# The V loads of an attention and two-MLP kernel, issued by GpSimd's queue instead of SyncE's

## The chip, the cores and the metric

The kernel runs on one core of one Trainium2 chip. The metric is the device time of one execution in microseconds (us), and shorter is better. Engines are named TensorE (PE), VectorE (DVE), ScalarE (ACT), GpSimd (POOL) and SyncE (SP). SyncE does no arithmetic here: it issues DMAs.

## The reference, cut to what matters

Chunked attention over 4 batch rows, 8 heads, 768 tokens and 64 dimensions, then two MLPs on the 3072 x 512 result, all in fp32:

```python
# per chunk c of 32 queries: 16 keys to the left, 8 to the right, 8 memory tokens in front
k_full = concat([mem_k, k[:, :, l_start:r_end]]); v_full = concat([mem_v, v[:, :, l_start:r_end]])
scores = q_c @ k_full.T / sqrt(D)
a = exp(scores - max(scores)); a = a / (sum(a) + 1e-9)
out[:, :, c] = a @ v_full
...
x = out.transpose(0, 2, 1, 3).reshape(3072, 512)
r = maximum(x @ w_in, 0)                                   # 512 -> 2048
x = (s * r * r + b) @ w_out                                # 2048 -> 512
g = x @ w_gate                                             # 512 -> 1536
y = (g * sigmoid(g) * (x @ w_val)) @ w_out2                # 1536 -> 512
```

## The kernel before

**Tiling.** The attention runs in 24 groups g of 128 queries (4 chunks, all 8 heads), six groups (GB) to a batch row. Three groups make one token tile of 384, which goes through the first MLP in slices W0 to W15 of 128 hidden units: `hp` is the slice's first product, `r` its ReLU, `ghi` and `glo` the two parts of s*r*r + b, `acc` the second product. fp32 accuracy comes from splitting each operand into a hi and a lo part and taking three matmuls for one (`product`, L559 to L562): hi weights times hi data, hi weights times lo data, lo weights times hi data, in this order. The third one needs the lo part of the weights.

**A slice of weights.** W15, for example, is 1 MB in two DMAs (L240 and L245, into a tile raw_first15 of the pool of "w" slots), then a split: a magnitude (L840 on ScalarE), two short VectorE steps (L846, L850), two long ones (L855, L862), the hi copy (L231) and lo (L904). The first 150 us hold the splits of all sixteen slices, beside the attention of the first groups.

**q and k.** The first six groups load whole token rows (`load_tokens`, L285) and transpose on TensorE (psQ, psK). Later ones load 36 to 44 small DMAs of 32 rows (`load_quadrant`, L327 to L350): K8 is the loads of group 8, into the tiles `kin` (one buffer for all groups) and `qin`. VectorE transposes them in blocks of 32 x 32: `qt` (L356) for queries, `kT` (L362) for keys. The next group's loads into kin wait for kT.

**V.** `load_values` (L378 to L405) writes a group's windows of V into one of two buffers, v0 or v1 by the group's parity: eight DMAs of 56 KB, ten or twelve at a batch row's ends. For the first two groups of a batch row it also loads the 8 rows of mem_v and copies them over the chunks with six GpSimd copies (L392). psV, or psB in later groups, is the matmul of the probabilities with V.

**What sets the order.** A planner (`Plan`, L63 to L143) simulates tasks with a cost each and starts, on every engine, the ready task with the longest way behind it; the instructions are then written in that order. A transfer is a task of SyncE (0.45 us for each DMA) followed by a task for the movement (`transfer`, L826). `LOADS` fixes the order of the first loads on SyncE: "W0 K0 W1 V0 K1 K2 W2 V1 W4 V2 ...". `plan_queries` (L929 to L956) places a group's loads. TensorE's order is written by hand (`START`, `VISITS`). Every engine runs its instructions strictly in order, and a DMA on SyncE waits for the one eight places ahead of it.

Of the kernel before, what the change touches and what calls it, by code (L numbers as in the profile page):

```python
# [41 lines left out]
}  # L42

LOADS = (
    "W0 K0 W1 V0 K1 K2 W2 V1 W4 V2 K3 W3 V3 K4 W6 K5 W5 V4 W8 V5 W7 W10 W9 "
)

MOVED = (
# [98 lines left out]
def attention_and_two_mlps(  # L147
# [21 lines left out]
    nc = tc.nc  # L169
    B, H, S, D = q.shape  # L170
    NT, DM = out.shape
    NMEM = mem_k.shape[2]
# [7 lines left out]
    GB = S // GQ  # L180
    T = 3 * GQ
    NC = GQ // CHUNK
    WIN = LEFT + CHUNK + RIGHT
    KC = NMEM + WIN
# [169 lines left out]
    def turn_queries(g):  # L354
        staged[g] = {"qt": ap_.tile([P, NP, GQ], F32, tag="qt", name=f"qt{g}")}
        nc.vector.transpose(  # L356
            out=staged[g]["qt"].rearrange("p j s -> p (j s)"), in_=loaded[g]["q"].rearrange("p j n i -> p (j n i)")
        )
# [19 lines left out]
    def load_values(g):  # L378

        b, gi = divmod(g, GB)  # L380
        s0 = gi * GQ
        n = g % 2
        if n not in v_bufs:
            v_bufs[n] = ld.tile([P, NC, NP, D], F32, tag=f"v{n}", name=f"v{n}")
        tv = v_bufs[n]
        for e in range(2):
            p0 = e * KC
            if gi < 2:
                mem = tv[p0:p0 + NMEM]
                nc.sync.dma_start(out=mem[:, 0], in_=mem_v[b, e:H:2].rearrange("h s d -> s h d"))  # L390
                for c in range(1, NC):
                    nc.gpsimd.tensor_copy(mem[:, c], mem[:, 0])  # L392
            for c in range(NC):
                a = s0 + c * CHUNK - LEFT
                left, over = max(0, -a), max(0, a + WIN - S)
                for row, first, n in (
                    (0, 0, left), (left, a + left, WIN - left - over), (WIN - over, S - over, over)
                ):
                    if n:
                        r0 = p0 + NMEM + row  # L400
                        nc.sync.dma_start(
                            out=tv[r0:r0 + n, c],
                            in_=v[b, e:H:2, first:first + n, :].rearrange("h s d -> s h d"),
                        )
        loaded.setdefault(g, {})["v"] = tv  # L405

    def bank(pool, tag, name):
# [393 lines left out]
    def second_store(h, s, i):  # L801
# [7 lines left out]
    plan = Plan(  # L809
        dict(w=SLOTS - LENT, wt=SLOTS - 2, fly=2),  # L810
        dict(
            sc=LENT, f=2, own=1, qk=1, v=2, kT=1, kt=1, qt=1, at=1, on=1, x=2, r=4, ghi=2, glo=2, acc01=1,
            acc2=1, acc3=1, a=2, h=2, yq=1, so=1, z=5, a1=1, a2=1, a3=1, v1=2, v2=1,
        ),
    )
# [10 lines left out]
    def transfer(deps, emit, n, kilobytes, get=(), take=(), give=(), rate=380.0, name=None):  # L826

        issue = issues[name] = plan.add(SP, 0.45 * n, emit, deps, [*get, "fly"], take=take)
        return plan.add(MOVE, kilobytes / rate, None, [issue], put=["fly"], lag=1.8, give=give)

    def split(landed, raw, key, pool, name, done, put=("w",), sums=False):

        held = {}
# [95 lines left out]
    def plan_queries(g, early):  # L929
        vv = None  # L930
        if g >= EARLY:
            qk = None
            for a in range(12):
                qk = transfer(
                    [issues[f"K{g}_{a - 1}"]] if a else [], lambda a=a: load_quadrant(g, *divmod(a, 3)), 4 if a % 3 else 1,
                    64 if a % 3 else 14, take=["qk"] if a == 0 else (), rate=100.0, name=f"K{g}_{a}",
                )
                if a == 5:
                    vv = transfer([], lambda: load_values(g), 8, 460, take=["v"], rate=180.0, name=f"V{g}")
            t = plan.add(DVE, 0.60, lambda: turn_queries(g), [qk], take=["qt"])  # L940
            at_[g] = {"v": vv, "qt": t}
            t = plan.add(DVE, 0.72, lambda: turn_keys(g), [t], take=["kT"], give=["qk"])
            t = plan.add(ACT, 0.82, lambda: spread_keys(ACT, g, False), [t], take=["kt"])
            t = either(f"m{g}", {ACT: 0.26, DVE: 0.20}, lambda e: spread_keys(e, g, True), [t], give=["kT"])
            at_[g]["t"] = at_[g]["qt"], t
            return
        qk = transfer(
            [], lambda: load_tokens(g), 4, 590, take=["sc"], rate=180.0, name=f"K{g}"
        )
        vv = transfer([], lambda: load_values(g), 8, 460, take=["v"], rate=180.0, name=f"V{g}")  # L950
        at_[g] = {"v": vv, "qk": qk}
        t = plan.add(PE, 0.44, lambda: stage_queries(g, early), [qk], take=["acc2"] if early else ["a"])
        at_[g]["qt"] = either(
            f"q{g}", {ACT: 0.50, DVE: 0.60}, lambda e: stage_queries_copy(e, g), [t], take=["qt"],
            give=["acc2"] if early else ["a"],
        )  # L956
# [277 lines left out]
    for item in START.split():  # L1234
        what, g = item[0], int(item[1:] or 0)
# [100 lines left out]
```

## Time and profile before

| | |
|---|---|
| device time, median of 3 runs | 1234.26 us (1233.92 to 1235.15) |
| profiled execution | 1235.41 us, of which the span is 1233.6 us |
| mean granted TensorE clock | 0.989 |
| TensorE busy (PE) | 1189.7 us, 96% of the span |
| VectorE busy | 773.4 us, 63% |
| ScalarE busy | 506.3 us, 41% |
| GpSimd busy | 22.8 us, 2% |
| V loads | 208 DMAs: 176 of 56 KB and, at a batch row's ends, 8 each of 48, 40, 16 and 8 KB; 16 more of mem_v, 8 KB each |

TensorE is the busiest engine, so what counts is where it waits: nearly all of it lies in the first 106 us, in which the weights are split and the first groups' attention runs. The loads of V end before 570 us. A row of the timeline reads: start, length, engine, line, operation, output <- input, count, and in brackets the idle time of the engine ahead of it with what ended it.

### The profile page before, as it was taken

To read this page: it belongs to the slowest core of one execution; us is meant where nothing else is said; L and a number is where in the kernel's file an instruction comes from. 1 tells how busy PE (TensorE), PEld (TensorE's weight loads), DVE (VectorE), ACT (ScalarE), POOL (GpSimd) and SP (SyncE) were. 2 spreads that over 40 slices of the span, in tenths; PEclk is the share of its full clock that TensorE was granted. 3 is DMA by queue.
4 is the path that set the end of the run, shared out by engine and by line. 5 is a ranking of instruction groups with operands and counts; after the bars stand their busy time and mean duration, and the time that the engine had idled before them with its cause. 6 is when DMAs were issued, how large, how long until landed. Compare 5 with 4: busy or idle time off the path is not lost.

```text
span 1233.6 us, 25831 instructions
## 1 busy us (share of the span) xinstructions
PE 1189.7 (96%) x10296; PEld 1129.8 (92%) x10296; DVE 773.4 (63%) x1496; ACT 506.3 (41%) x1018; POOL 22.8 (2%) x54
## 2 busy tenths in 40 slices
PE   3788999999999999999999999999999999999998
PEld 3677999999999999999999999999999999999997
DVE  5899975556445444543679886658864448744444
ACT  2455433331334333333367555445543335433332
POOL 1001100000000000000000000000000000000000
PEclk9799999999999999999999999999999999999999
DMA  8956442223222232230462555567755458554532
GB/s 191 219 120 190 104 123 43 62 52 67 44 51 63 42 67 45 51 91 1 156 219 96 187 198 188 188 227 282 263 187 187 183 182 299 207 186 188 188 114 93
DMA packets 217128, 174.11 MB, mean 141 GB/s; under 512 B 157487, under 2 KB 188719, under 8 KB 215471
## 3 DMA queue, kind: packets, MB, share of 16 engines
q1 hardware_dynamic: 217006, 172.45, 45.1%
q8 instruction: 81, 1.33, 0.4%
q14 instruction: 41, 0.33, 0.1%
HBM read 124.40 MB, written 47.97 MB: 140 GB/s over the span
## 4 chain that ended last, share of the span: by engine, by line
PE 79%; SPq 9%; DMA 6%; DVE 3%; issue 2%; ACT 1%; DVEq 0%; ACTq 0%
PE chain_a L560 6%; PE chain_a L561 6%; PE chain_a L562 6%; PE oacc L561 5%; PE oacc L560 5%; PE oacc L562 5%; PE acc L560 5%; PE acc L561 5%; PE acc L562 5%; PE hp L560 5%; PE hp L562 5%; PE hp L561 5%; PE chain_b L561 4%; PE chain_b L562 4%; PE chain_b L560 4%; SPq L350 3%
## 5 line engine op out<-in xcount | busy, mean ns | idle before, releaser
L560 PE MATMUL acc<-ghi,w_first 128*128 128x384 f32 x512 | 176.0, 344 | 3.0 <-DVE ghi L231 1.8
L560 PE MATMUL hp<-xhi,w_first 128*128 128x384 f32 x512 | 175.7, 343 | 0.7 <-ACT xhi L229 0.7
L561 PE MATMUL acc<-glo,w_first 128*128 128x384 f32 x512 | 173.2, 338 | 2.5 <-DVE glo L622 1.1
L561 PE MATMUL hp<-xlo,w_first 128*128 128x384 f32 x512 | 172.6, 337 | 1.1 <-DVE xlo L553 1.1
L562 PE MATMUL hp<-xhi,w_first 128*128 128x384 f32 x512 | 172.5, 337 | 0.0
L562 PE MATMUL acc<-ghi,w_first 128*128 128x384 f32 x512 | 172.3, 337 | 0.0
L748 ACT ACTIVATE kept<-chain_a 128x256 f32<-128x256 f32 x216 | 83.0, 385 | 163.4 <-PE chain_a L562 134.4
L600 DVE SCALAR_TENSOR_TENSOR r<-r,s_sb 128x384 f32<-128x384 f32 x92 | 57.0, 620 | 107.8 <-ACT r L589 105.1
L589 ACT ACTIVATE r<-hp 128x384 f32<-128x384 f32 x96 | 47.1, 491 | 186.1 <-PE hp L562 179.1
L560 PE MATMUL oacc<-w_down,ghi 128*128 128x512 f32 x288 | 114.1, 396 | 0.1
L561 PE MATMUL oacc<-w_down,ghi 128*128 128x512 f32 x288 | 114.1, 396 | 0.0
L562 PE MATMUL oacc<-w_down,glo 128*128 128x512 f32 x288 | 112.0, 389 | 0.0
L560 PEld LDWEIGHTS acc<-ghi,w_first 128*128 128x128 f32 x512 | 96.8, 189 | 5.9 <-DVE ghi L231 2.8
L561 PEld LDWEIGHTS acc<-glo,w_first 128*128 128x128 f32 x512 | 97.0, 189 | 5.4 <-DVE glo L620 3.1
L560 PEld LDWEIGHTS hp<-xhi,w_first 128*128 128x128 f32 x512 | 97.3, 190 | 2.2 <-ACT xhi L229 0.9
L561 PEld LDWEIGHTS hp<-xlo,w_first 128*128 128x128 f32 x512 | 97.4, 190 | 1.3 <-DVE xlo L553 1.3
L562 PEld LDWEIGHTS hp<-xhi,w_first 128*128 128x128 f32 x512 | 97.1, 190 | 0.0
L562 PEld LDWEIGHTS acc<-ghi,w_first 128*128 128x128 f32 x512 | 96.8, 189 | 0.0
L765 DVE TENSOR_TENSOR v<-v,g 128x256 f32<-128x256 f32 x144 | 61.0, 424 | 52.3 <-ACT g L761 50.4
L753 DVE TENSOR_TENSOR v<-chain_b,kept 128x256 f32<-128x256 f32 x144 | 61.0, 423 | 41.5 <-PE chain_b L562 26.8
L773 DVE TENSOR_TENSOR glo<-v,ghi 128x256 fp32r<-128x256 f32 x144 | 60.6, 421 | 36.6 <-ACT ghi L229 36.6
L560 PE MATMUL chain_a<-y,hi_up 128*128 128x256 f32 x288 | 81.3, 282 | 0.6 <-ACT kept L748 0.5
(137 smaller groups left out, 2689.4 us busy)
## 6 DMA issues: line engine op xcount, KB each, us to landing
y<-ops_dram SPq DMA_DIRECT2D x48, 512.0 KB
ops_dram<-y SPq DMA_DIRECT2D x24, 512.0 KB
sum_dram<-o SPq DMA_DIRECT2D x48, 256.0 KB
o<-sum_dram SPq DMA_DIRECT2D x12, 1024.0 KB
v<-in_v_dram SPq DMA_DIRECT2D x176, 56.0 KB
yhi<-ops_dram_hi SPq DMA_DIRECT2D x12, 768.0 KB
ylo<-ops_dram_lo SPq DMA_DIRECT2D x12, 768.0 KB
raw_first<-in_moe_w_in_dram SPq DMA_DIRECT2D x16, 512.0 KB
```

Source lines behind the costliest of these rows:

```text
L350: nc.sync.dma_start(out=qin[:, j], in_=q[b, h, s0:s0 + GQ, ds].rearrange("(n t) i -> t n i", t=QUAD))
L560: nc.tensor.matmul(o, whi, xhi, start=first, stop=False, skip_group_check=onto)
L561: nc.tensor.matmul(o, whi, xlo, start=False, stop=False, skip_group_check=onto)
L562: nc.tensor.matmul(o, wlo, xhi, start=False, stop=last, skip_group_check=onto)
L589: nc.scalar.activation(out=r, in_=hp, func=AF.Relu)
L600: nc.vector.scalar_tensor_tensor(out=r, in0=r, scalar=s_sb[:, 0:1], in1=r, op0=ALU.mult, op1=ALU.mult)
L748: nc.scalar.activation(out=t, in_=st2[n]["A"], func=AF.Copy)
L753: nc.vector.tensor_tensor(out=t, in0=st2[n]["B"], in1=st2[n].pop(f"a{i}"), op=ALU.add)
L765: nc.vector.tensor_tensor(out=v, in0=v, in1=g, op=ALU.mult)
L773: nc.vector.tensor_tensor(out=lo, in0=st2[n].pop(f"v{half + 1}"), in1=st2[n][f"hi{half}"].bitcast(F32), op=ALU.subtract)
```

## The change

All DMAs of `load_values` are issued by `nc.gpsimd`. GpSimd's copies of mem_v move behind the DMAs of their group. The planner no longer counts V as a transfer of SyncE: a new function `load_v` makes it a task of POOL with 1.0 us for each DMA, and a movement of its own; the V names leave `LOADS`.

```diff
--- before.py
+++ after.py
@@ -42,7 +42,7 @@
 }
 
 LOADS = (
-    "W0 K0 W1 V0 K1 K2 W2 V1 W4 V2 K3 W3 V3 K4 W6 K5 W5 V4 W8 V5 W7 W10 W9 "
+    "W0 K0 W1 K1 K2 W2 W4 K3 W3 K4 W6 K5 W5 W8 W7 W10 W9 "
 )
 
 MOVED = (
@@ -387,9 +387,7 @@
             p0 = e * KC
             if gi < 2:
                 mem = tv[p0:p0 + NMEM]
-                nc.sync.dma_start(out=mem[:, 0], in_=mem_v[b, e:H:2].rearrange("h s d -> s h d"))
-                for c in range(1, NC):
-                    nc.gpsimd.tensor_copy(mem[:, c], mem[:, 0])
+                nc.gpsimd.dma_start(out=mem[:, 0], in_=mem_v[b, e:H:2].rearrange("h s d -> s h d"))
             for c in range(NC):
                 a = s0 + c * CHUNK - LEFT
                 left, over = max(0, -a), max(0, a + WIN - S)
@@ -398,10 +396,14 @@
                 ):
                     if n:
                         r0 = p0 + NMEM + row
-                        nc.sync.dma_start(
+                        nc.gpsimd.dma_start(
                             out=tv[r0:r0 + n, c],
                             in_=v[b, e:H:2, first:first + n, :].rearrange("h s d -> s h d"),
                         )
+        for e in range(2 if gi < 2 else 0):
+            mem = tv[e * KC:e * KC + NMEM]
+            for c in range(1, NC):
+                nc.gpsimd.tensor_copy(mem[:, c], mem[:, 0])
         loaded.setdefault(g, {})["v"] = tv
 
     def bank(pool, tag, name):
@@ -827,6 +829,11 @@
 
         issue = issues[name] = plan.add(SP, 0.45 * n, emit, deps, [*get, "fly"], take=take)
         return plan.add(MOVE, kilobytes / rate, None, [issue], put=["fly"], lag=1.8, give=give)
+
+    def load_v(g):
+        edge = 4 * (g % GB == 0) + 2 * (g % GB in (1, GB - 1))
+        issue = plan.add("POOL", 1.0 * (8 + edge), lambda: load_values(g), take=["v"])
+        return plan.add("MOVE_V", 0.1, None, [issue], lag=2.0)
 
     def split(landed, raw, key, pool, name, done, put=("w",), sums=False):
 
@@ -936,7 +943,7 @@
                     64 if a % 3 else 14, take=["qk"] if a == 0 else (), rate=100.0, name=f"K{g}_{a}",
                 )
                 if a == 5:
-                    vv = transfer([], lambda: load_values(g), 8, 460, take=["v"], rate=180.0, name=f"V{g}")
+                    vv = load_v(g)
             t = plan.add(DVE, 0.60, lambda: turn_queries(g), [qk], take=["qt"])
             at_[g] = {"v": vv, "qt": t}
             t = plan.add(DVE, 0.72, lambda: turn_keys(g), [t], take=["kT"], give=["qk"])
@@ -947,7 +954,7 @@
         qk = transfer(
             [], lambda: load_tokens(g), 4, 590, take=["sc"], rate=180.0, name=f"K{g}"
         )
-        vv = transfer([], lambda: load_values(g), 8, 460, take=["v"], rate=180.0, name=f"V{g}")
+        vv = load_v(g)
         at_[g] = {"v": vv, "qk": qk}
         t = plan.add(PE, 0.44, lambda: stage_queries(g, early), [qk], take=["acc2"] if early else ["a"])
         at_[g]["qt"] = either(
```

The planner places other work in answer. On SyncE at the start, the first rows behind W0 and K0 (numbers at a name's end tell buffers apart; v0 is group 0's V, qk1 the rows of group 1). Before:

```order
L240 DMA raw_first1_162<-in_moe_w_in_dram 128x4x256
L245 DMA raw_first1_162<-in_moe_w_out_dram 128x1024
L390 DMA v0_167<-in_mem_v_dram 8x4x64
L401 DMA v0_167<-in_v_dram 16x4x64
L401 DMA v0_167<-in_v_dram 40x4x64
L401 DMA v0_167<-in_v_dram 56x4x64 x3
```

And after:

```order
L240 DMA raw_first1_181<-in_moe_w_in_dram 128x4x256
L245 DMA raw_first1_181<-in_moe_w_out_dram 128x1024
L285 DMA qk1_186<-in_mem_k_dram 8x8x64
L285 DMA qk1_186<-in_k_dram 72x8x64
L285 DMA qk1_186<-in_q_dram 128x8x64
L285 DMA qk1_186<-in_k_dram 80x8x64
```

V0 is gone from between W1 and K1, the rows of group 1.

The V loads stand on GpSimd instead, from the program's start; these are its first rows after the change:

```order
masks.py:197 MEMSET ident_81 128x128
L390 DMA v0_156<-in_mem_v_dram 8x4x64
masks.py:199 ISA
masks.py:199 AFFINE_SELECT ident_81<-ident_81 128x128
L399 DMA v0_156<-in_v_dram 16x4x64
L399 DMA v0_156<-in_v_dram 40x4x64
L399 DMA v0_156<-in_v_dram 56x4x64 x3
```

Before, GpSimd held nothing there but the identity's making and the copies of mem_v.

On SyncE in the middle of the loads of group 8 (kin and qin8), where W15 (raw_first15) is issued. Before, where 14 of the group's 36 loads stand ahead of W15:

```order
L346 DMA kin_872<-in_k_dram 32x4x32
L350 DMA qin8_1855<-in_q_dram 32x4x32
L240 DMA raw_first15_1936<-in_moe_w_in_dram 128x4x256
L245 DMA raw_first15_1936<-in_moe_w_out_dram 128x1024
L346 DMA kin_872<-in_k_dram 32x4x32
```

And after, where 27 of the 36 stand ahead:

```order
L346 DMA kin_503<-in_k_dram 32x4x32
L350 DMA qin8_1866<-in_q_dram 32x4x32
L240 DMA raw_first15_2009<-in_moe_w_in_dram 128x4x256
L245 DMA raw_first15_2009<-in_moe_w_out_dram 128x1024
L327 DMA kin_503<-in_k_dram 24x4x32
```

W15 has moved back by 13 loads of group 8.

On VectorE at the end of the weights' splits: w_first15 is W15's hi (CAST) and lo (TENSOR_TENSOR), on6 the attention's output of group 6, psS7 and sc7 the scores of group 7, qt8 and kT8 the transposes of group 8. Before:

```order
L531 TENSOR_TENSOR on6_2085<-psV6_1_2023,rc6_1932 128x4x64
L622 SCALAR_TENSOR_TENSOR glo_2088<-r_2012,b_sb_87,ghi_2081 128x384
L231 CAST w_first15_2132<-raw_first15_1936 128x1024
L600 SCALAR_TENSOR_TENSOR r_2083<-r_2083,s_sb_86 128x384
L904 TENSOR_TENSOR w_first15_2132<-raw_first15_1936,w_first15_2132 128x1024
L622 SCALAR_TENSOR_TENSOR glo_2150<-r_2083,b_sb_87,ghi_2142 128x384
L468 TENSOR_REDUCE mx7_2165<-psS7_0_2098 128x4
L468 TENSOR_REDUCE mx7_2165<-psS7_1_2099 128x4
L481 TENSOR_TENSOR sc7_2170<-psS7_0_2098,mx7_2165 128x4x64
L481 TENSOR_TENSOR sc7_2170<-psS7_1_2099,mx7_2165 128x4x64
L356 STREAM_TRANSPOSE qt8_2173<-qin8_1855 128x512
L362 STREAM_TRANSPOSE kT8_2176<-kin_872 128x640
```

And after (L853, L857, L862 and L869 are the old L846, L850, L855 and L862):

```order
L483 TENSOR_TENSOR sc7_2141<-psS7_0_2082,mx7_2129 128x4x64
L483 TENSOR_TENSOR sc7_2141<-psS7_1_2083,mx7_2129 128x4x64
L624 SCALAR_TENSOR_TENSOR glo_2149<-r_2116,b_sb_87,ghi_2131 128x384
L853 TENSOR_SCALAR t_first15_2143<-t_first15_2143 128x1024
L857 TENSOR_SCALAR t_first15_2143<-t_first15_2143 128x1024
L862 SCALAR_TENSOR_TENSOR raw_first15_2009<-raw_first15_2009,t_first15_2143 128x1024
L869 SCALAR_TENSOR_TENSOR raw_first15_2009<-raw_first15_2009 128x1024
L356 STREAM_TRANSPOSE qt8_2156<-qin8_1866 128x512
L231 CAST w_first15_2158<-raw_first15_2009 128x1024
L362 STREAM_TRANSPOSE kT8_2160<-kin_503 128x640
L911 TENSOR_TENSOR w_first15_2158<-raw_first15_2009,w_first15_2158 128x1024
```

W15's split, done before sc7 in the old order, begins behind sc7 in the new one and ends behind kT8. TensorE's rows stand in the same order in both kernels.

## Rows read from the trace of the kernel before

**Rows 1.** Stretches: busy us of PE, PEld, DVE, ACT, POOL; PEclk; DMA share; GB/s.
```profile
0.00:60.00 60.00, 33.12 (x560) 28.30 (x561) 43.12 (x78) 19.87 (x31) 5.00 (x18) 0.86 0.87 201
60.00:150.00 90.00, 81.60 (x803) 75.57 (x802) 86.07 (x136) 46.07 (x70) 8.46 (x12) 0.96 0.54 147
150.00:270.00 120.00, 119.83 (x1290) 116.57 (x1289) 74.27 (x152) 38.93 (x67) 0.00 (x0) 1.00 0.31 68
276.00:280.00 4.00, 4.00 (x17) 4.00 (x16) 0.56 (x1) 1.35 (x3) 0.55 (x2) 0.61 0.30 55
```

**Rows 2.** Timeline near 274 us, TensorE and VectorE: start, length, operation, [idle before <-releaser].
```profile
274.56 0.44 PE L560 MATMUL acc<-ghi,w_first 128*128 128x384 f32 x1 [1.63 <-DVE ghi L231]
...
272.23 0.71 DVE L356 STREAM_TRANSPOSE qt<-qin 128x512 f32<-128x512 f32 x1 [3.33 <-DMA v<-in_mem_v_dram]
```

**Rows 3.** SyncE's queue ahead of that wait.
```profile
245.71 4.21 SPq L401 DMA_DIRECT2D v<-in_v_dram  x10
...
270.20 0.43 SPq L350 DMA_DIRECT2D qin<-in_q_dram  x1
```

**Rows 4.** TensorE in the first 50 us.
```profile
18.50 1.09 PE L415 MATMUL psQ<-ident,qk 128*128 128x128 f32 x4 [5.59 <-DMA qk<-in_q_dram]
19.38 1.06 PE L495 MATMUL psA<-ident,qk 128*128 128x128 f32 x4
42.53 1.26 PE L511 MATMUL psV<-v,at 64*32 64x64 f32 x64 [0.78 <-DVE at L231]
```

**Rows 5.** SyncE's queue in the first 40 us.
```profile
14.80 0.46 SPq L285 DMA_DIRECT2D qk<-in_q_dram  x1
29.81 7.36 SPq L401 DMA_DIRECT2D v<-in_v_dram  x8
```

**Rows 6.** ScalarE, group 0's exponential.
```profile
14.87 0.63 ACT L488 ACTIVATE qk<-qk 128x512 f32<-128x512 f32 x1 [1.28 <-DVE qk L481]
```

**Rows 7.** VectorE from 141 to 197 us, the steps around W15, kT and qt.
```profile
141.02 0.75 DVE L481 TENSOR_TENSOR sc<-psS,mx 128x256 f32<-128x256 f32 x2
145.37 0.83 DVE L362 STREAM_TRANSPOSE kT<-kin 128x640 f32<-128x640 f32 x1
159.95 0.69 DVE L846 TENSOR_SCALAR t_first<-t_first 128x1024 f32<-128x1024 f32 x1 [2.24 <-ACT t_first L840]
165.41 0.69 DVE L231 CAST w_first<-raw_first 128x1024 fp32r<-128x1024 f32 x1
166.54 1.22 DVE L904 TENSOR_TENSOR w_first<-raw_first,w_first 128x1024 fp32r<-128x1024 f32 x1
169.53 0.71 DVE L356 STREAM_TRANSPOSE qt<-qin 128x512 f32<-128x512 f32 x1
170.15 0.81 DVE L362 STREAM_TRANSPOSE kT<-kin 128x640 f32<-128x640 f32 x1
...
190.13 0.20 DVE L526 RECIPROCAL rc<-rc 128x8 f32<-128x8 f32 x1
196.39 0.70 DVE L356 STREAM_TRANSPOSE qt<-qin 128x512 f32<-128x512 f32 x1
```

**Rows 8.** SyncE's queue: K8's first load, W15's second, K8's last.
```profile
146.23 0.30 SPq L327 DMA_DIRECT2D kin<-in_k_dram  x1
153.86 0.50 SPq L245 DMA_DIRECT2D raw_first<-in_moe_w_out_dram  x1
166.06 0.43 SPq L350 DMA_DIRECT2D qin<-in_q_dram  x1
```

**Rows 9.** ScalarE, W15's magnitude.
```profile
158.80 1.12 ACT L840 ACTIVATE t_first<-raw_first 128x1024 f32<-128x1024 f32 x1 [1.74 <-DMA raw_first<-in_moe_w_out_dram]
```

**Rows 10.** TensorE, the first product with W15's lo.
```profile
168.35 0.33 PE L562 MATMUL hp<-xhi,w_first 128*128 128x384 f32 x1
```

**Rows 11.** GpSimd's copies over the span (ns: min/median/max); VectorE beside one.
```profile
L392 POOL COPY v<-v x48: 386/393/1408, 12.4 to 447.5; 8x256 f32<-8x256 f32 x48
...
114.44 1.41 DVE L862 SCALAR_TENSOR_TENSOR raw_first<-raw_first 128x1024 uint32<-128x1024 uint32 x1
```

## The prediction

> **What bounds the kernel now.** I read the stretches first, then the engines inside them. After 570 us no V is loaded and nothing in the change differs, so only the first 570 us count. In 0 to 60 us TensorE is busy 33 of 60 us and the DMA engines 0.87; in 60 to 150 us TensorE lacks 8.4 of 90 us while VectorE is busy 86; from 150 to 270 us TensorE is busy 119.83 of 120 [rows 1]. Past 150 us a stall of TensorE therefore goes into the total in full, and time saved on another queue saves nothing unless TensorE waited for it. Its one large wait there is 1.63 us at 274.56 for a split of r, after VectorE had sat 3.33 us ahead of qt [rows 2]. The page puts that to a DMA of V, but the instruction reads qin; ahead of its 44 loads, the last issued at 270.20, stood ten V loads on SyncE, 4.21 us [rows 3]. Before 60 us the wait that V's place in the queue can explain is psQ's 5.59 us at 18.50 [rows 4]: its q is issued at 14.80, behind V0's twelve loads [rows 5].
>
> **The change part by part. V off SyncE.** It frees 224 issues, but the prize is small. At the start K1's q could go out earlier; psA stands behind psQ and needs an exponential that would still end at 15.50 [rows 6], while psA now starts right behind psQ's four matmuls, at 19.38 [rows 4]. So the gain is 0 to 3.9 us. Against it stands the DMA share of 0.87: V0 now asks for the same engines at the same time. I take 1.0, nearer the DMA-bound end. On that the Trainium skill, "DMA: Bandwidth & Descriptors", section "Issuing engines are not separate DMA queues", says that issuing from several engines saves only the sequencer's time, usually little; by it alone this term would be 0, and the 0.87 here agrees with it.
>
> **The order that comes with it.** This is the part that decides. The planner, told that SyncE no longer carries V, also moves W's loads and splits; PE's order stays the same. In the order before, W15 (the last slice of the first MLP's weights) is issued after 14 of K8's 36 small loads, in the order after, behind 27 of them. K8 cannot start before kT7 has been read out of kin, the one buffer: kT7 ends at 145.37 + 0.83 = 146.20 and K8's first load goes out at 146.23 [rows 7, 8]. Its first 14 took until 153.4, W15's second issue ended at 153.86 + 0.50 = 154.36, and the other 22 ended at 166.49, 0.55 each [rows 8]. On VectorE neighbours overlap by up to 0.09 (qt takes 0.71, but kT follows 0.62 later [rows 7]); the steps below are counted with it. Step by step:
> - kT7. After sc6 (141.02, 0.75 long [rows 7]) VectorE now has two W steps (1.22 long, 1.14 with the overlap), three steps of r, 1.6 together (an estimate from the 0.4 to 0.6 that each takes alone), one more W step, qt and kT: 3 × 1.14 + 1.6 + 0.63 + 0.8 = 6.45 from 141.69, so kT7 ends at 148.1, 1.9 us later than now. TensorE's order fixes sc6 itself, so I leave that where it is.
> - K8's 27 loads: 7.2 us for 14, then 13 × 0.55 = 7.2, so 162.5. W15's two issues take 0.95: 163.45.
> - W15's landing: ACT's magnitude started on it at 158.80 [rows 9], 4.44 after 154.36: 167.9.
> - The magnitude, 1.15 to the next step's start at 159.95 [rows 7]: 169.05. Then the two short steps (0.73 apart) and the two long ones (1.14): 3.74; qt8, which now stands between them and the hi copy, 0.63; the copy 0.60; kT8 0.76; and lo, 1.22 [rows 7]. Together 6.95: lo is ready at 176.0.
> - TensorE's first product that needs lo stands at 168.35, the third of hp, whose first stands 0.35 ahead [rows 10]. Now lo ends at 166.54 + 1.22 = 167.76, with 0.6 us in hand; after the change it is **7.6 us late**. The hi copy, ready at 169.05 + 3.74 + 0.63 + 0.69 = 174.1, makes some 6 us of it ahead of the first product; the rest comes before the third.
> - The clock. After the 1.63 us wait the granted clock in 276 to 280 us is 0.61 [rows 1], so for the most part at the 1.2 GHz level: at 0.61 of full speed these 4 us do the work of 2.4, and 1.6 us are lost. I take 1.5 here, since part of a shortfall may fall into the second wait. Bounds 0 and 1.8.
>
> The W15 term's lower bound: the landing without V's traffic in 3 us, two thirds of 4.44 (an estimate from that row alone): 6.2. The upper: 9, if SyncE's ring of eight outstanding DMAs holds the 27 loads up by three times half a microsecond more.
>
> **K9 and the later qt.** In the order after, qt9 stands right behind the reciprocal that ends at 190.33, 6 us earlier on VectorE than now (196.39 [rows 7]), and there it would wait for its loads. K8's 36 with W15 took 20.3 us (146.23 to 166.49 [rows 8]); K9's, with four stores of y among them, take about 21, and 1.6 more to land, as K12's last (issued by 270.63, read at 272.23 [rows 2, 3]). From kT8's new end, 174.8, that is 197.4. VectorE would reach qt9 at 190.4 in the old time, plus the 9 us that TensorE is late by then: 199.4. So this wait is hidden, but only behind the W15 stall; were W15 in time, it would cost some 5 us by itself. The two are not added. At qt12 it is alike: K12's 44 loads no longer wait for V, but qt12 now stands before the evacuation of hp into r and no longer behind it. The saving there is between 3.2 (1.63 of wait, 1.6 of clock) and a loss of 1; I take 0, since the loop of 44 loads, landing, qt and kT (from 249.92 to 270.63 they took 20.7 [rows 3]; 20.7 + 1.6 + 1.5 = 23.8) nearly fills one group's 25 us.
>
> **GpSimd.** It issues instead of SyncE. No row shows what one such DMA costs its engine. Its copies of mem_v take 0.39 at the median and 1.41 at the longest [rows 11], which are my bounds; V2's eight loads took 7.36 / 8 = 0.92 each on SyncE's ring [rows 5], which I take. At 0.92, V0 to V2 (30 DMAs, 12 copies of 0.39, 2 us to land) are in by 1 + 27.6 + 4.7 + 2 = 35.3, and psV needs V2 at 42.53 [rows 4]: hidden. VectorE's steps lengthen while GpSimd works, 1.41 [rows 11] where a W step takes 1.22 [rows 7]. About 48 loads fall into the saturated stretch, up to 0.12 us lost at each: 0 to 5.5 us. I take 0.5, because from 106 us on TensorE, by the busy share of [rows 1], hardly waits for VectorE.
>
> **Sum.** 7.6 + 1.5 − 1.0 + 0.5 + 0 = +8.6 us. On the profiled execution (1235.41 us, 1.8 of it outside the span of 1233.6) that is 1244.0; that execution lies 1.15 above the median, so against the median 1234.26 it is **1242.9 us**.
>
> **The rivals.**
> - Faster. W15 isn't late, because its loads or K8's run ahead of my count (SyncE's ring no longer waits for V's 56 KB loads, and kT7 comes earlier), or TensorE is already held up before it. Then 1.0 at the start and 3.2 at 274 remain: 1234.3 − 1.0 − 3.2 = 1230.1. For it: V was the largest traffic beside K8. Against it: 27 issues behind one kin buffer take 27 × 0.43 = 11.6 us at the least [rows 8], and W15 has 0.6 in hand. It decides if W15's lo ends before 168.4, 7.6 us earlier than counted. Chance 0.13.
> - GpSimd too slow. At 1.41 us per DMA V2 is in at 1 + 42.3 + 4.7 + 2 = 50.0, 7.5 us late for psV; from 1.16 each, (42.5 − 7.7) / 30, it costs. With W15's loss that gives 1250.4. Chance 0.10.
> - GpSimd and VectorE in each other's way: 5.5 us where I took 0.5, 1247.9. The Trainium skill, "SBUF — State Buffer", section "Who interferes with whom", speaks against this change: GpSimd writes the descriptors of the DMAs that it issues through a port pair that it shares with VectorE, and during some of VectorE's operations it is locked out. A copy of 1.41 against the median of 0.39 agrees with such a lock for copies; for DMAs no run here shows it. Chance 0.10.
> - No change. The W15 term at its lower end, the clock lost for 0.4 only, the whole gain at the start and at 274: 1234.3 + 6.2 + 0.4 − 3.9 − 3.2 + 0.5 = 1234.3. Chance 0.10.
>
> **How the numbers follow.** The forecast itself has 0.57 and runs from 1238 to 1247 with its terms' bounds. About 0.2% (2.5 us) is what a measurement of this kernel can tell from no change, so faster is below 1231.8 and slower above 1236.7. Faster: 0.13, the first rival. Within: 0.10, the last. Slower: the rest, 0.77. The range leaves out the faster rival and little else: 1233.5 to 1250.5.
>
> **What would show it.** In the changed profile: W15's two loads on SyncE near 162 to 164 us with K8's on both sides; ACT's magnitude at 168 waiting for them; TensorE waiting 6 to 8 us at hp, in two pieces, for W15's hi copy and lo, and after it a granted clock well under 1; K1's q out before 12 us, but psA not before 15.5; V2 complete before 42. I am wrong if TensorE passes 165 to 185 us without a wait, if a wait of its own for V appears in the first 50 us, or if qt9 holds VectorE.

## The result and the profile after

The changed kernel takes **1247.58 us** (median of four runs, 1244.88 to 1249.59) against 1234.70 for the kernel before in the same comparison: a ratio of 1.0107, 95% interval 1.0089 to 1.0125, slower by 12.9 us where 8.6 were predicted. The time lies in the range of 1233.5 to 1250.5. The sum came near the truth partly because two errors offset each other.

The profiled execution, the slowest of the four, has a span of 1247.8 us. Its stretches, in the columns of [rows 1]:

```profile
0.00:60.00 60.00, 31.91 (x551) 27.17 (x552) 43.85 (x78) 19.51 (x31) 37.88 (x64) 0.86 1.03 197
60.00:150.00 90.00, 76.73 (x769) 71.81 (x768) 75.89 (x123) 40.95 (x63) 28.45 (x44) 0.92 0.55 149
150.00:270.00 120.00, 113.94 (x1117) 110.08 (x1116) 74.37 (x141) 41.30 (x70) 21.51 (x34) 0.96 0.30 67
180.00:188.00 8.00, 7.02 (x21) 6.51 (x22) 4.65 (x10) 1.44 (x2) 0.00 (x0) 0.51 0.16 25
```

GpSimd is now busy 38 of the first 60 us, and the DMA share (the time that the packets took) is 1.03 after 0.87, at about the same GB/s. From 60 to 150 us TensorE is busy 4.9 us less than before and VectorE 10.2 less: VectorE isn't slower, it stands idle. From 150 to 270 us TensorE, busy 119.83 of 120 before, is now busy 113.94.

TensorE runs the same instructions in the same order in every kernel told of here, so each instruction's start can be set against its start in the kernel before. The difference, in us, shows where the time goes. The columns are TensorE instructions, named by their start in the kernel before: 130.46 lies behind the splits of W5 to W10, 196.03 behind W15, 316.89 behind the wait of [rows 2], 549.75 near the end of V's loads. The last column is the median of all runs, the ratio that to the kernel before in the same comparison, where that kernel's median lay between 1233.91 and 1235.39.

| kernel (profiled execution) | 130.46 | 196.03 | 316.89 | 549.75 | median us, ratio (interval) |
|---|---|---|---|---|---|
| after | +7.1 | +16.6 | +12.9 | +14.1 | 1247.58, 1.0107 (1.0089 to 1.0125) |
| e1_v_alone | −0.6 | −0.6 | −3.0 | −3.3 | 1231.68, 0.9979 (0.9963 to 0.9996) |
| e2_w5_first | +8.2 | +17.0 | +13.3 | +14.4 | 1250.08, 1.0111 (1.0084 to 1.0137) |
| e3_w15_first | +3.5 | +12.5 | +9.6 | +10.2 | 1245.93, 1.0087 (1.0070 to 1.0104) |
| e4_both | +9.0 | +17.4 | +14.5 | +16.9 | 1248.42, 1.0111 (1.0086 to 1.0135) |
| e5_bytes_back | +2.1 | +12.4 | +12.3 | +14.7 | 1248.46, 1.0102 (1.0071 to 1.0132) |
| e6_bytes_and_issue | +1.9 | +1.1 | −0.5 | +1.7 | 1238.09, 1.0017 (1.0000 to 1.0034) |
| e7_order_alone | +12.4 | +21.4 | +26.0 | +27.9 | 1262.85, 1.0216 (1.0199 to 1.0233) |
| e8_w15_split_first | +5.4 | +10.2 | +6.6 | +9.1 | 1243.59, 1.0058 (1.0040 to 1.0075) |
| e9_loads_early | +4.6 | +13.6 | +10.7 | +11.7 | 1247.31, 1.0097 (1.0077 to 1.0118) |
| e10_magnitudes_late | +4.2 | +12.3 | +8.2 | +10.9 | 1246.48, 1.0097 (1.0074 to 1.0120) |
| e11_all_places | −1.1 | +4.3 | +0.5 | +2.6 | 1238.93, 1.0042 (1.0024 to 1.0061) |

So the change loses 7.1 us before 130 us, 9.1 more around W15 (from +7.4 at 157.16 to +16.6), and gets 3.7 back at the wait of [rows 2]. The first column spreads: after, e3 and e8 have the same orders up to there and show +7.1, +3.5 and +5.4. Differences of up to 3.6 us in it prove nothing.

**The early loss.** Two of TensorE's waits from 60 to 150 us, the first of them its longest there; the kernel before has none at these places:

```profile
78.89 1.09 PE L497 MATMUL psA<-ident,qk 128*128 128x128 f32 x4 [4.14 <-DVE on L533]
...
87.93 0.30 PE L513 MATMUL psV<-v,at 64*32 64x64 f32 x2 [1.05 <-ACT kt L229]
```

ScalarE behind them, with the magnitudes of W5 and then of W7 and W8 (two in one row):

```profile
74.58 1.12 ACT L847 ACTIVATE t_first<-raw_first 128x1024 f32<-128x1024 f32 x1 [8.98 <-DMA raw_first<-in_moe_w_out_dram]
75.59 0.63 ACT L490 ACTIVATE qk<-qk 128x512 f32<-128x512 f32 x1
85.14 2.19 ACT L847 ACTIVATE t_first<-raw_first 128x1024 f32<-128x1024 f32 x2 [2.81 <-DMA kin<-in_k_dram]
87.23 1.08 ACT L229 ACTIVATE kt<-psK 128x448 f32<-128x448 f32 x3
```

ScalarE stands 8.98 us ahead of W5's magnitude, with group 4's exponential queued behind it; then it stands again ahead of those of W7 and W8, with the copies of group 5's keys behind them. The page puts the second wait to kin, but the instruction reads raw_first. In the chain of waits (start, length, what) W7's first load takes 12.52 us to land, at 83.41; the last 1.70 us ahead of the magnitude the chain, too, puts to kin.

```profile
70.27 0.51 SPq L245
70.89 12.52 DMA raw_first<-in_moe_w_in_dram
```

These lengths are those of one execution. In e3 and e8, whose orders are the same up to there, ScalarE stands only 2.56 and 2.69 us ahead of W5's magnitude and not at all ahead of those of W7 and W8, and TensorE has no wait at psA; still they are late by 3.5 and 5.4 us at 130 us. e3:

```profile
69.66 1.15 ACT L847 ACTIVATE t_first<-raw_first 128x1024 f32<-128x1024 f32 x1 [2.56 <-DMA raw_first<-in_moe_w_out_dram]
```

In the kernel before, W5 is issued at 57.43 and W8 and W7 stand further back in ScalarE's order, behind group 5's keys. Now W5 comes out at 67.58, behind 22 small loads of K6, which SyncE could not issue at once: some of them had to wait for an older DMA. From 46 to 62 us (waits on SyncE's queue: us in total, times, longest):

```profile
SPq L350 <- DMA qk<-in_k_dram: 3.3, 1, 3.3
SPq L350 <- DMA raw_first<-in_moe_w_out_dram: 2.5, 1, 2.5
SPq L346 <- DMA raw_first<-in_moe_w_in_dram: 1.8, 1, 1.8
```

**W15.** TensorE waits at W15's first product for the hi copy and at the third for lo:

```profile
180.12 0.69 PE L562 MATMUL hp<-xhi,w_first 128*128 128x384 f32 x1 [5.06 <-DVE w_first L231]
...
181.99 0.69 PE L564 MATMUL hp<-xhi,w_first 128*128 128x384 f32 x1 [0.85 <-DVE w_first L911]
```

VectorE there:

```profile
172.55 0.62 DVE L602 SCALAR_TENSOR_TENSOR r<-r,s_sb 128x384 f32<-128x384 f32 x1 [1.99 <-ACT r L591]
...
173.75 0.74 DVE L483 TENSOR_TENSOR sc<-psS,mx 128x256 f32<-128x256 f32 x2
174.41 0.60 DVE L624 SCALAR_TENSOR_TENSOR glo<-r,b_sb,ghi 128x384 fp32r<-128x384 f32 x1
174.94 0.68 DVE L853 TENSOR_SCALAR t_first<-t_first 128x1024 f32<-128x1024 f32 x1
...
179.42 0.65 DVE L231 CAST w_first<-raw_first 128x1024 fp32r<-128x1024 f32 x1
...
180.75 1.18 DVE L911 TENSOR_TENSOR w_first<-raw_first,w_first 128x1024 fp32r<-128x1024 f32 x1
```

No row between r and lo has a wait: the split runs back to back, behind a step that waits for TensorE's own previous slice. W15's second load had been issued at 168.41, and ScalarE came to the magnitude (173.73) without idling. But the load had only just landed: the one eight places behind it, which waits for it, went out at 173.65.

### The profile page after: what moved, and what is told of

Same layout as the page of the kernel before. It is cut to its first block, busy times and chain, and to the rows that moved or that the text cites. A ratio compares the mean times of both kernels' runs of the same rounds, so it can differ in the third digit from the quotient of the medians.

```text
span 1247.8 us, 25838 instructions
## 1 busy us (share of the span) xinstructions
PE 1193.1 (96%) x10296; PEld 1133.2 (91%) x10296; DVE 773.8 (62%) x1496; ACT 505.8 (41%) x1018; POOL 169.1 (14%) x278
## 4 chain that ended last, share of the span: by engine, by line
PE 81%; DVE 7%; SPq 5%; DMA 4%; issue 2%; ACT 1%; DVEq 0%; ACTq 0%
PE hp L562 6%; PE acc L563 6%; PE acc L562 6%; PE hp L564 6%; PE chain_a L562 6%; PE acc L564 6%; PE hp L563 6%; PE chain_a L563 5%; PE chain_a L564 5%; PE oacc L563 5%; PE oacc L562 5%; PE oacc L564 5%; PE chain_b L563 4%; PE chain_b L564 4%; PE chain_b L562 4%
## 5 line engine op out<-in xcount | busy, mean ns | idle before, releaser
L562 PE MATMUL hp<-xhi,w_first 128*128 128x384 f32 x512 | 177.7, 347 | 5.7 <-DVE w_first L231 5.1
L564 PE MATMUL hp<-xhi,w_first 128*128 128x384 f32 x512 | 174.1, 340 | 0.9 <-DVE w_first L911 0.9
L399 POOL DMA_DIRECT2D v<-in_v_dram x208 | 132.4, 644 | 308.1 <-PE psB L513 202.6
```

What stands on the lines that cost most here:

```text
L399: nc.gpsimd.dma_start(out=tv[r0:r0 + n, c], in_=v[b, e:H:2, first:first + n, :].rearrange("h s d -> s h d"),)
L562: nc.tensor.matmul(o, whi, xhi, start=first, stop=False, skip_group_check=onto)
L564: nc.tensor.matmul(o, wlo, xhi, start=False, stop=last, skip_group_check=onto)
```

## The experiments

### V's queue alone

The kernel before with its own order on TensorE, VectorE and ScalarE; only V's loads move to GpSimd, and the mem_v copies behind them. The planner still believes that SyncE issues V.

```diff
-                nc.sync.dma_start(out=mem[:, 0], in_=mem_v[b, e:H:2].rearrange("h s d -> s h d"))
+                nc.gpsimd.dma_start(out=mem[:, 0], in_=mem_v[b, e:H:2].rearrange("h s d -> s h d"))
...
-                        nc.sync.dma_start(
+                        nc.gpsimd.dma_start(
                             out=tv[r0:r0 + n, c],
```

> The kernel before with one edit: the V loads go out on GpSimd's queue (mem_v's copies behind their group's loads), while the planner still counts V on SyncE, so that the work on TensorE, VectorE and ScalarE stands in the order before. Theory A (the loss comes from the order that the planner makes once V is off SyncE): this kernel is faster than before by what the wait at 274 us cost, 3.2 us and perhaps 0.6 at 422: 1230 to 1232. Rival B (issuing by GpSimd costs the time, by slower loads of V or by holding up VectorE): 1239 to 1248, most of the 13 us lost. Rival C: V's place doesn't matter, 1233 to 1236.

1231.68 us, 0.9979 of the kernel before: a gain of some 3 us that is just past the 0.2%. Most of it (2.5 us, between 196.03 and 316.89 in the table) lies at the wait of [rows 2], which is 0.94 us now, and behind which the granted clock is 1.00 (275 to 279 us) instead of 0.61:

```profile
273.30 0.44 PE L562 MATMUL acc<-ghi,w_first 128*128 128x384 f32 x1 [0.94 <-DVE ghi L231]
```

VectorE's long steps from 60 to 150 us (count, busy us, mean ns), with GpSimd issuing beside them, are what they were in the kernel before (1239 and 1218 there):

```profile
L864 DVE SCALAR_TENSOR_TENSOR raw_first<-raw_first 128x1024 uint32<-128x1024 uint32 x12 | 14.7, 1237 | 0.1
L906 DVE TENSOR_TENSOR w_first<-raw_first,w_first 128x1024 fp32r<-128x1024 f32 x11 | 13.3, 1218 | 0.0
```

So the move as such doesn't cost: neither GpSimd's slower issue nor its neighbourhood with VectorE. What costs is the order that the planner makes of it.

### The order alone

The counterpart: after's order on TensorE, VectorE and ScalarE word for word, V's loads back on SyncE at the places that the plan's times give.

```diff
-                nc.gpsimd.dma_start(out=mem[:, 0], in_=mem_v[b, e:H:2].rearrange("h s d -> s h d"))
+                nc.sync.dma_start(out=mem[:, 0], in_=mem_v[b, e:H:2].rearrange("h s d -> s h d"))
...
-                        nc.gpsimd.dma_start(
+                        nc.sync.dma_start(
                             out=tv[r0:r0 + n, c],
```

> Edit: the orders of PE, VectorE and ScalarE are those of after, word for word, but V's loads are issued by SyncE again, at the places in its queue that the plan's times give (V0 behind W0, V1 behind K2, and so on). Only the queue differs from after. Theory P: the order is what costs, so the time is not better than after: 1246 to 1256 us, worse than after since SyncE's queue has V's issues in it again. Rival Q (GpSimd's queue is what costs): the time goes back to 1233 to 1237 us.

1262.85 us, worse than either and above the 1246 to 1256 expected. The four kernels make a square (medians):

| | V on SyncE | V on GpSimd |
|---|---|---|
| order of before | 1234.7 | 1231.7 |
| order of after | 1262.9 | 1247.6 |

GpSimd's queue gains 3.0 us under the old order and 15.3 under the new one; the new order costs 28.2 us on SyncE's queue and 15.9 on GpSimd's. The stretches of e7 show a loss from the start:

```profile
0.00:60.00 60.00, 28.54 (x539) 24.18 (x540) 39.53 (x73) 15.01 (x24) 9.41 (x18) 0.80 0.80 188
60.00:150.00 90.00, 75.76 (x752) 69.93 (x750) 74.72 (x117) 44.44 (x68) 6.47 (x12) 0.91 0.54 154
```

Part of it is V's place on SyncE and not the order of the other engines: V0's twelve loads stand ahead of K0 in e7, and TensorE's first matmul starts at 13.10 us, in after at 8.94. The 28.2 and the 15.3 us hold this place too. The clean pair is e1 and after: both have V on GpSimd, only the order differs, and it costs 15.9 us.

### W5's and W15's loads, by SyncE's order

Three kernels change nothing but SyncE's order in after, one list of names each: W5's two loads ahead of the 22 small loads of K6, W15's two behind 10 of K8's instead of 27, and both.

```diff
-        for t in plan.run():
+        started = plan.run()
+        for name, ahead in (("W5", "K6_1"), ("W15", "K8_4")):
+            t = issues[name]
+            started.remove(t)
+            started.insert(started.index(issues[ahead]), t)
+        for t in started:
```

> The changed kernel with one edit: W5's two loads go out ahead of 22 of K6's small loads instead of behind them and K5; the rest of SyncE's queue and all the other engines' orders are those of the changed kernel. Theory A (ScalarE's 9 us of waiting for W5 at 74.6 us, with group 4's exponential and r queued behind it, makes the loss before 100 us): W5's magnitude starts near 66 instead of 74.6, TensorE's wait of 4.1 us at psA (78.9) goes, and the time falls by 4 to 8 us, to 1240 to 1244. Rival: the early loss is VectorE's order or GpSimd's traffic: unchanged within 2 us, 1246 to 1249.

> The changed kernel with one edit: W15's two loads go out behind 10 of K8's small loads instead of 27. Theory P (the prediction's: W15 lands too late): ScalarE's magnitude of W15 and TensorE's hp move forward by 5 us or more, and with the clock 7 to 9 us are won: 1238.5 to 1241. Theory V (VectorE's order: W15's split stands behind group 7's scores, which wait for TensorE, so the landing isn't what is waited for): unchanged within 1.5 us, 1246 to 1249, with TensorE's waits of 5.1 and 0.9 us at W15's hp still there.

> The changed kernel with both edits of the two runs before: W5's loads ahead of 22 of K6's, W15's behind 10 of K8's. If the two are separate causes, the gains of those runs add; by theory V for W15 this equals the run with W5 alone within 1.5 us.

None gains clearly: 1250.08, 1245.93 and 1248.42, for 1247.58. In e2 W5's magnitude has no wait any more, but ScalarE then stands 8.92 us ahead of W7's and W8's, and group 5's keys come as late as in after:

```profile
65.41 1.16 ACT L847 ACTIVATE t_first<-raw_first 128x1024 f32<-128x1024 f32 x1
...
85.19 2.15 ACT L847 ACTIVATE t_first<-raw_first 128x1024 f32<-128x1024 f32 x2 [8.92 <-DMA kin<-in_k_dram]
```

In e3 W15 is in much earlier, and TensorE waits for it as long as before:

```profile
176.55 0.69 PE L562 MATMUL hp<-xhi,w_first 128*128 128x384 f32 x1 [5.06 <-DVE w_first L231]
```

After, e2, e3, e9 and e10 all wait 5.06 us there and e4 5.07, whatever the lateness they arrive with. A landing would not give the same hundredth five times; a fixed row of VectorE instructions does. That W15's landing alone holds the split is refuted: in e3 the loads go out 11.5 us earlier. So is my guess that W5's lateness alone makes the early loss. In after itself landing (by 173.65) and place (173.73) meet, so that there either would have held the split; no run moves the split and leaves the loads late.

### W15's split by VectorE's order

After, with W15's loads as in e3, and its split moved on ScalarE and VectorE: magnitude, bound, shift, sign and rest ahead of on6, hi and lo ahead of mx7 and sc7 (`marks` remembers the plan's tasks of a slice and of a stage).

```diff
+        w15 = marks["W15"]
+        on6, mx7 = plan.tasks[marks["on6"]], plan.tasks[marks["mx7"]]
+        for t, ahead in ((issues["W15"], issues["K8_4"]), *((t, on6) for t in w15[:5]), *((t, mx7) for t in w15[5:])):
+            started.remove(t)
+            started.insert(started.index(ahead), t)
```

> Edit: after, with W15's two loads behind 10 of K8's, and W15's split moved ahead in the orders of ScalarE and VectorE: magnitude, bound, shift, sign and rest ahead of on6, hi and lo ahead of mx7 and sc7, about where they stand in the kernel before. Nothing else moves. Theory V: the waits of 5.06 and 0.85 us at W15's first products go, with the half clock behind them, and the time falls by 5 to 9 us against after, to 1238 to 1243 us: 1238 if the later wait of VectorE at qt9 costs nothing, 1243 if it costs the 5 us that the prediction put on it were W15 in time. Theory L (landing): no change, 1245 to 1249 us, as for the loads moved alone.

1243.59 us, 4.0 less than after: a smaller gain than the 5 to 9 us expected, and just past the 1243. The two waits at W15 are gone, and from 170 to 180 us the granted clock is 1.00. What remains of the loss (4.5 us between 157.16 and 196.03 instead of 9.1) comes with two new waits: on6 now stands behind the split, and psS7 waits for on6; and 18 us later TensorE waits for an r.

```profile
172.35 1.17 PE L459 MATMUL psS<-kt,qt 64*32 64x64 f32 x64 [2.11 <-DVE on L533]
...
190.49 0.44 PE L562 MATMUL hp<-xhi,w_first 128*128 128x384 f32 x1 [1.28 <-DVE r L593]
```

Neither is qt9, which the prediction had put there at 5 us; VectorE waits 1.03 us for its loads, and TensorE not at all:

```profile
200.59 0.71 DVE L356 STREAM_TRANSPOSE qt<-qin 128x512 f32<-128x512 f32 x1 [1.03 <-DMA qin<-in_q_dram]
```

### V's bytes given back to the planner

`load_v` books V on a movement of its own with 0.1 us; in the kernel before V took 2.56 us of the movement that all loads share. e5 gives that back (the second pair of lines); e6 also puts the 0.65 us that the trace shows in place of the 1.0 us for a DMA of GpSimd.

```diff
-        issue = plan.add("POOL", 1.0 * (8 + edge), lambda: load_values(g), take=["v"])
-        return plan.add("MOVE_V", 0.1, None, [issue], lag=2.0)
+        issue = plan.add("POOL", 0.65 * (8 + edge), lambda: load_values(g), take=["v"])
+        return plan.add(MOVE, 460 / 180.0, None, [issue], lag=1.8)
```

> Edit: V's loads stay on GpSimd's queue, but the planner counts their 460 KB as time of its transfer resource again (2.56 us for each group, as before), so that it no longer takes the loads of K and W for earlier than they are. The weights stand in SyncE's order as W6, W5, 18 of K6, W8, W7 instead of W6, 22 of K6, W5, W8, W7, and the magnitudes of the weights move back in ScalarE's order with them; W15's loads still stand behind 27 of K8's and its split behind sc7 on VectorE. Theory P (the early loss comes from an order that the planner made with V's bytes left out): the +7 to +10 us at 77 to 130 us goes to within 2 us of the kernel before, the +9 at W15 stays, so 1238 to 1242 us. Rival Q (the early loss comes from GpSimd's queue or from the fuller DMA engines, whatever the order): the +7 stays and the time is 1246 to 1250 us.

> Edit: e5_bytes_back, and the planner's 1.0 us for one DMA issued by GpSimd is 0.65 us, as the trace of after shows it. In the order that comes out of this W15's loads stand behind 9 of K8's and its split ahead of sc7 on VectorE, as in the kernel before. Theory P with theory V (W15's loss is its place behind sc7): both losses go, and the time is 1229 to 1236 us, at or below the kernel before. Rival Q: the early +7 stays, 1238 to 1242 us. Rival L (W15 is late for another reason than its place): the 5-us wait at W15's first matmul stays, 1238 to 1242 us.

By its time alone e5 (1248.46) would speak against the theory; its table row says otherwise. The early loss is down to +2.1, about the 2 us expected and below the +3.5 to +7.1 of the kernels with after's early order, and between 60 and 90 us ScalarE waits ahead of no magnitude. But its order puts W15's split behind the reciprocal of group 7 as well, and the magnitude behind group 7's exponential, and W15 costs 10.6 us there. 1.6 of them are a landing after all: ScalarE waits 1.64 us for W15's second load (issued at 163.73), and VectorE behind it 1.63.

```profile
169.52 0.69 DVE L524 TENSOR_REDUCE rc<-sc 128x8 f32<-128x512 f32 x1 [0.17 <-ACT sc L490]
...
171.13 1.12 ACT L847 ACTIVATE t_first<-raw_first 128x1024 f32<-128x1024 f32 x1 [1.64 <-DMA raw_first<-in_moe_w_out_dram]
...
172.28 0.69 DVE L853 TENSOR_SCALAR t_first<-t_first 128x1024 f32<-128x1024 f32 x1 [1.63 <-ACT t_first L847]
...
177.01 0.69 PE L562 MATMUL hp<-xhi,w_first 128*128 128x384 f32 x1 [7.62 <-DVE w_first L231]
```

And the gain at [rows 2] is gone, with a wait of 3.04 us for r behind a late qt. In e6's order the split stands ahead of sc7, as in the kernel before: no loss at W15, 1238.09 us in all, within 0.2% of the kernel before. That is 2 us above the 1229 to 1236 expected, and by its time alone it would fit rival Q; but Q held that the early loss stays at 7 us, and it is +1.9. TensorE from 150 to 200 us:

```profile
150.00:200.00 50.00, 50.00 (x531) 48.88 (x530) 34.65 (x68) 16.77 (x28) 10.55 (x16) 1.00 0.39 96
```

The plan's own times, which the program computes, show why. Issue times in us, planned and in the trace:

| | W5 plan | W5 real | W8 plan | W8 real | W7 plan | W7 real |
|---|---|---|---|---|---|---|
| before | 50.9 | 57.43 | 66.9 | 74.83 | 71.4 | 81.41 |
| after | 50.2 | 67.58 | 53.7 | 69.85 | 57.1 | 70.89 |
| e5_bytes_back | 48.1 | 54.50 | 62.6 | 67.94 | 63.5 | 70.08 |
| e6_bytes_and_issue | 48.1 | 54.06 | 63.8 | 68.61 | 64.7 | 69.65 |

The planner was 6.5 to 10.0 us too early before and is 13.8 to 17.4 too early after; with V's bytes back it is 4.8 to 6.6 too early. It places the magnitudes where it believes the loads to be in.

### The two early places

e9 sets SyncE's early order back (K5, W5 ahead of 15 loads of K6, W8 and W7 behind them), e10 only ScalarE's and VectorE's (the magnitudes of W7 and W8 and two short steps on W7 behind group 5's keys and the next r). e11 does both, and e8's move. The first loop is in e9 and e11, the second in e10 and e11.

```diff
+        for name, ahead in (("K5", "K6_1"), ("W5", "K6_1"), ("W8", "K6_5"), ("W7", "K6_5")):
+            t = issues[name]
+            started.remove(t)
+            started.insert(started.index(issues[ahead]), t)
+        w7, w8 = marks["W7"], marks["W8"]
+        for t in (*w7[:3], w8[0]):
+            started.remove(t)
+            started.insert(started.index(w7[3]), t)
```

> Edit: after, with only SyncE's order changed between 45 and 72 us: K5 and W5 ahead of 15 of K6's small loads instead of behind 22, W8 and W7 behind those 15, as in the kernel before. The orders of ScalarE and VectorE stay, with the magnitudes of W7 and W8 ahead of the copies of kt5. Theory G (two gates in a row, the loads' order on SyncE and the magnitudes' place on ScalarE, and either holds TensorE by itself): still +7 us or more at 88 to 130 us, 1244 to 1249 us. Theory S (SyncE's order alone makes the early loss): within 2 us of the kernel before at 130 us, 1238 to 1242 us.

> Edit: after, with only ScalarE's and VectorE's orders changed: the magnitudes of W7 and W8 and two of VectorE's steps on W7 move behind the copies of kt5, xhi and the next r, about where they stand in the kernel before. SyncE's order stays, with W5 behind 22 of K6's loads. Theory G: the waits for W5 stay (+6 us at 73 us) while the one at psV (88 us) shrinks; +4 to +7 us at 130 us, 1243 to 1248 us. Theory A (the magnitudes' place alone makes the early loss): within 2 us of the kernel before at 130 us, 1238 to 1242 us.

> Edit: e9's and e10's moves together with those of e8 (W15's loads and split), so that the three places found in the trace stand as in the kernel before; everything else is after, V on GpSimd's queue included. Theory G with theory V: both losses go and the time is 1231 to 1238 us, some 10 to 15 us under after. If another part of the order costs as much, 1240 us or more.

One at a time they leave +4.6 (+7 or more was expected of e9) and +4.2 at 130.46, which the spread of that column doesn't tell from after, and times of 1247.31 and 1246.48. Together the early loss is gone (−1.1) in the profiled execution. From 60 to 150 us e11's TensorE is as busy as in the kernel before (81.60 in [rows 1]):

```profile
60.00:150.00 90.00, 81.27 (x816) 76.22 (x815) 83.78 (x137) 46.48 (x70) 27.89 (x44) 0.98 0.54 144
165.85 1.49 PE L459 MATMUL psS<-kt,qt 64*32 64x64 f32 x64 [2.10 <-DVE on L533]
```

e11 takes 1238.93 us, 8.7 less than after, one more than I had allowed; e8's wait at psS7 is still in it. Against e8, which has the same moves at W15, it gains 4.7 us; but two of its ten runs took 1243.59 and 1244.98, and the intervals of the two ratios overlap. So, as far as one trace of each kernel tells, the early loss has two gates, the loads' place on SyncE and the magnitudes' place on ScalarE, and opening one alone shows nothing. The version that beats both kernels is e1, the change without its new order, though by 0.2% only.

## Why the prediction came out as it did

- **The order decides: right.** The prediction named the order that comes with the change as its deciding part, and e1 beside after shows it; e7 points the same way. The rival that made GpSimd too slow (V2 late, 1250.4) is refuted: a V load takes GpSimd 0.64 us, below the 0.92 taken, V2's last one is issued by 31.7 us, and no wait for V appears.
- **W15: right size by luck, one step wrong.** 7.6 + 1.5 = 9.1 us were predicted and 9.1 lost (16.6 − 7.4), but the waits come to 5.91 us (5.06 + 0.85) instead of 7.6, and the clock takes the rest. Up to K8's first load the count held: it went out at 155.54 and not at 148.1, and these 7.4 us are the early loss. The step that failed is "W15's landing": the sum let the split wait for W15's loads and for nothing else. VectorE's order has the split behind sc7, and sc7 behind a chain that TensorE's previous slice feeds. e3 moves the loads and keeps the 5.06 us; e8 moves loads and split and loses them. In after the landing came at the same moment as the place, so the sum was near for the wait of that trace, without having its cause.
- **The clock: mis-sized.** 1.5 us were taken with an upper bound of 1.8. The granted clock is 0.51 from 180 to 188 us, the 1.2 GHz level for nearly all of it. TensorE's shift goes from +12.1 at 168.00 to +16.4 at 172.16; less 0.85 of wait that is some 3.5 us. The row that the term was taken from had 4 us at 0.61, behind a single wait.
- **The early stretch: missed.** The sum had −1.0 + 0.5 there, and +7.1 came in the profiled execution. The prediction read SyncE's order at the start and around W15, but not between 45 and 72 us, where W5 to W8 had moved against K6's loads and against ScalarE's order. A diff of the orders shows it at once; the prediction went to the one place with the longest count.
- **The start: the gain is 0.** psQ starts at 18.41 after 18.50, though K1's q goes out at 7.49 instead of 14.80. The Trainium skill, "DMA: Bandwidth & Descriptors", section "Issuing engines are not separate DMA queues", says that issuing from several engines saves only the sequencer's time, and by that this term was 0: the trace agrees (−0.09, in e1 −0.23). The same section calls that time usually small; under the old order the whole move is worth 3.0 us. The 15.3 us between e7 and after are no test of it, since they hold V0's place ahead of K0.
- **274 us: a gain of 3.7, predicted 0** with bounds of −3.2 and +1. qt12 waits 0.35 us instead of the 3.33 of [rows 2], and TensorE's clock stays at 1.00 from 289 to 293 us, behind the same instruction, where [rows 1] has 0.61 from 276 to 280.
- **qt9: 1 us, and not TensorE's.** The prediction held that it would cost 5 us were W15 in time. In e8 and e11 W15 is in time, VectorE waits 1.03 and 0.99 us for qt9's loads, and TensorE doesn't wait there. The loop was sized right: from kT8's end to qt9 it took 22.4 and 22.9 us, for 21 + 1.6 counted. VectorE came to qt9 21.3 and 21.9 us behind kT8, where a wait of 5 would have it there after some 17.6.
- **GpSimd and VectorE.** 0.5 us were taken, up to 5.5 allowed, from 48 loads of 0.12 us (that is 5.8, and no row shows the 0.12). The step of 1.41 us in [rows 11] from which the prediction took that VectorE lengthens while GpSimd works stands beside GpSimd's copies, and beside V's DMAs VectorE's long steps are as short as ever (1.22 us, below). From 60 to 150 us the three long ones of a split take 1241, 1216 and 1234 ns in after, for 1222, 1239 and 1218 in the kernel before. The lock of which the Trainium skill, "SBUF — State Buffer", section "Who interferes with whom", speaks may be there for the copies, which themselves go from 492 ns in the mean to 597; its price for TensorE is not measurable here.

Without the early loss the change would have lost 12.9 − 7.1 = 5.8 us or so (an estimate, since the first is a difference of medians and the second of one execution each; with the +3.5 of e3, 9.4); without the gain at 274, 3.7 more. These two, both outside their terms, offset each other in part.

What stays open: why the early column spreads by up to 3.6 us between kernels with equal orders there, which of its many small waits carries e9's and e10's remaining 4 us, and what W15 would cost with the split alone moved ahead.

## What to carry to other kernels

When a change takes work off a resource that a planner models, the larger effect may be the order that the planner then makes: measure the move with the old order held and the order with the old place held, four kernels in a square, before blaming the hardware. A load on another queue still moves its bytes (the DMA share of the first 60 us did not fall, 1.03 after 0.87), so they must stay in the plan. On engines that run in order, a wait that is removed may stand in front of the next one; test such gates together, and test whether a wait is a landing or a place by moving only the loads: if it stays the same to the hundredth, a place holds it. Then move the place alone as well, since the landing may stand right behind it.

## What the runs showed of the hardware

- A V load keeps GpSimd busy for 0.64 us in the mean; on SyncE ten of them took 4.21 us, 0.42 each [rows 3].

```profile
L399 POOL DMA_DIRECT2D v<-in_v_dram x208 | 132.4, 644 | 308.1 <-PE psB L513 202.6 <-PE psV L513 89.0 <-DMA v<-in_v_dram 11.6
```

- GpSimd's copies lengthen VectorE's steps beside them, its DMA issues don't. Of the two long uint32 steps of each split in the first 160 us of after and e1, the ten beside copies take 1.22 to 1.42 us, the fifteen that lie for over half of their time beside DMA issues 1.19 to 1.23, and the 31 with nothing on GpSimd beside them 1.18 to 1.23. One beside copies, in after:

```profile
113.87 5.76 POOL L406 COPY v<-v 8x256 f32<-8x256 f32 x6
...
117.96 1.41 DVE L862 SCALAR_TENSOR_TENSOR raw_first<-raw_first,t_first 128x1024 uint32<-128x1024 uint32 x1
```

- The clock does not follow the length of one wait. After 5.06 us it was 0.51 for 8 us, after 7.62 in e5 it was 0.63 from 177 to 185, after 1.63 in the kernel before 0.61 for 4 us; after 2.11 in e8 it was 1.00 from 170 to 180, and after 2.10 in e11 0.79 from 164 to 172.
- Small loads on SyncE wait for large ones ahead of them: between 46 and 62 us in after, SyncE spent 7.6 us ahead of loads of K6, 16 KB each, waiting for DMAs of W6 and K4, of 512 and some 150 KB, and W5 stood behind them.
